# An attention, mixture and MLP kernel on one core: row sums inverted in groups of two head pairs instead of by batch, and two more pairs with split scores

## The chip, the core and the metric

The kernel runs on one core of a Trainium2 chip. Its time is device time in microseconds (us). The core has five engines: TensorE (PE; weight loads are listed apart as PEld), VectorE (DVE), ScalarE (ACT), GpSimd (POOL) and SyncE (SP), which here issues nearly all DMAs. Each engine works through its own instructions in order and waits on semaphores for the others. PE reads from SBUF and writes to PSUM; a DMA moves data between DRAM and SBUF, or inside SBUF.

## What is computed

Three stages follow each other; the output of one is the input of the next.

```python
# 1. attention: q, k, v are [4, 12, 448, 64]
scores = cap * np.tanh(scale * np.matmul(q, k.transpose(0, 1, 3, 2)) / cap)
attn = np.exp(scores - np.max(scores, axis=-1, keepdims=True))
attn = attn / (np.sum(attn, axis=-1, keepdims=True) + 1e-09)
x = np.matmul(attn, v)                    # heads side by side: [4, 448, 768]
# 2. mixture of 4 experts, 2 by token; each is causal attention with 64 columns
a = softmax(where(causal, -1e9, scale * (x @ wq[e]) @ (x @ wk[e]).T))
out += mask[..., None] * w[:, :, kk:kk + 1] * (a @ (x @ wv[e]) @ wo[e])
# 3. gated MLP on out
h = gelu(out @ w_in); u, v = halves(h); v_n = layernorm(v) * g_ln
y = out + (u * (einsum('ts,bsd->btd', w_sg, v_n) + b_sg[None, :, None])) @ w_out
```

The work around the change is the division in the third line of stage 1 and the matrix product of stage 1's first line.

## The kernel before

**Tiling.** There are four batches of 448 tokens (`B`, `S`). Stage 1 goes by pairs of heads: six pairs a batch (`HP`), 24 in all. `slot(i, side)` does pair `i`'s scores beside pair `i-1`'s values. Scores of 128 keys by 448 queries come in blocks; `p` is tanh of a block and then exp, both on ACT. `pb` adds up the blocks of `p` of a pair (DVE, on POOL for some of the later pairs). `values` multiplies `p` by v into `po`, and ACT copies that to `os`, one tile for each group of two pairs.

**The division.** `sums(b, i)` adds up `pb` over its partitions with a matmul by a matrix of ones, for group `i` (0, 1, 2) of batch `b`. With `onehot` it puts the sums of group `i` into row `i` of four blocks of 32 rows, and collects the three groups of a batch in one tile `rs`: ACT copies the first, DVE adds the others. When the batch is complete, `invert` writes `rs` to DRAM (`rd`), `spread` reads it back with four DMAs so that it lies across all partitions (`ri`, 128x42), `inverted` takes the reciprocal on DVE and writes it to DRAM with four DMAs, and `load_rb` reads it twice for each group, repeated over 64 partitions each time (`rb`). `over_sums` multiplies `os` by `rb` on DVE. `in_parts` then makes `xh` (rounded to F32R) and `xl` (what is left), from which stage 2's matmuls `qk` and `v` read. `normed(n, place)` says at which place of which slot each of these steps is recorded.

**Split scores.** From pair `PARTED` on, q and k are first split into a rounded half and a rest (`qh`, `ql`, `kh`, `kl`, in `part`), and a block of scores is three F32R products instead of one in F32 (`block`). The last 64 keys (`tails`) stay in F32 for all pairs.

**What sets the order.** The program is recorded in three parts and each is ordered by a planner in the kernel (`Agenda`): it gives each instruction a duration, lets it start when its inputs, its engine and its buffers are there, and writes every engine's instructions in the order that comes out. Part 1 is slots 0 to 9 with the preparation of `w_in` beside them (`wi` tiles on DVE and ACT, `w2ps` matmuls on PE); part 2 is slots 10 to 24, with stage 2 of the earlier batches beside them (`PLAN`); part 3 is the rest of stage 2 and stage 3. `Agenda.SLACK` is added to each DMA's landing in the first two parts, and `Agenda.MARGIN` (one number for them, one for the third) to what PE waits for from elsewhere. SP's DMAs go by the same plan, so a DMA that waits for a semaphore holds those behind it.

**Other names.** `W_OUT` says at which slots the five first units of `w_out` are prepared, and in which buffers. `experts_end` records the end of stage 2, with the division of the last batch among it. In the rows every operation has line 448, the helper that records them all; the tile names tell them apart.

Of the kernel before, what the change touches and what calls it, by code (L numbers as in the profile page):

```python
# [76 lines left out]
class Agenda:  # L77


    LATENCY = {"pe": 230.0, "act": 60.0, "dve": 60.0, "pool": 100.0, "sp": 60.0}  # L80
    SLACK, MARGIN = 0.0, (0.0, 100.0)
    STATE = ("slots", "queue", "where", "left", "free", "grid", "fresh", "cfg", "bank", "lock", "pipe", "kept")
    RULES = ((100.0, 0.0, 100.0), (100.0, 0.0, None), (100.0, 20.0, 100.0), (60.0, 0.0, 100.0))
    OVERLAP = {"act": 100.0, "dve": 80.0, "pool": 27.0, "sp": 0.0}
# [334 lines left out]
def build(ctx: ExitStack, tc: tile.TileContext, a: dict):  # L419
# [40 lines left out]
    def dma(*args, **kw):  # L460
        return sp.dma_start(*args, **kw) if agenda.on else nc.sync.dma_start(*args, **kw)
# [6 lines left out]

    capt = const.tile([128, 1], F32, name="capt")
    tsc = const.tile([128, 1], F32, name="tsc")  # L470
    onehot = const.tile([128, 3, 32], F32, name="onehot")
    tri = const.tile([128, E, E], F32, name="tri")
    ident = const.tile([128, 128], F32, name="ident")
    mhalf = const.tile([128, 1], F32, name="mhalf")
# [1 line left out]

    def constants(pool):
        negf = pool.tile([128, 128 + KT], F32, name="negf", bufs=1)
        dma(onehot, a["c_onehot"])
        dma(ident, a["c_ident"])  # L480
        dma(negf, a["c_neg"])
        dma(tri, a["c_tri"])
        pool_e.memset(neg, 0.0)
        return negf
# [63 lines left out]
            dma(qp, a["qT"][b, :, hp, :])  # L548
        return qp, kp, load_v(b, hp)

    PARTED = 14

    parts = {}

# [94 lines left out]
    def sums(b, i):  # L649
        g = ps_g.tile([128, 512], F32, tag="g", name=f"sum{b}_{i}")  # L650
        for j in range(4):
            mm(g[32 * j:32 * j + 32, :S], onehot[:, i, :], pend[b, 2 * i + j // 2][2][:, j % 2, :],
                             start=True, stop=True)
        if i == 0:
            sums_t[b] = ao.tile([128, S], F32, name=f"rs{b}", tag="rs", bufs=1)
            act.activation(sums_t[b], g[:, :S], AF.Copy)
        else:
            dve.tensor_tensor(sums_t[b], sums_t[b], g[:, :S], op=ALU.add)
        yield 870.0

    def invert(b):
        d, n = dr.tile([4, 32, S], F32, tag="rd", name=f"rd{b}"), 3 * S // 32
        dma(d.rearrange("j r s -> (j r) s"), sums_t[b])
        rows = d[:, :3, :].rearrange("j r s -> j (r s)").rearrange("j (p c) -> j p c", c=n)
        r = ao.tile([128, n], F32, name=f"ri{b}", tag="ri", bufs=1)
        inv[b] = (r, rows)
        rb_d[b] = d

    def spread(b):
        r, rows = inv[b]  # L670
        for j in range(4):
            dma(r[32 * j:32 * j + 32], rows[j])

    def inverted(b):
        r, rows = inv.pop(b)
        dve.reciprocal(r, r)
        for j in range(4):
            dma(rows[j], r[32 * j:32 * j + 32])

    pairs = [(b, hp) for b in range(B) for hp in range(HP)]  # L680
    ld = {}
# [1 line left out]
    def slot(i, side):  # L683

        if i == 0:
            ld[0] = load_pair(*pairs[0])
            ld[1] = load_pair(*pairs[1])
        if i + 2 < len(pairs):  # L690
            qk = [at.tile([128, n], F32, tag=t, name=f"{t}{i + 2}", bufs=3) for t, n in (("qp", S), ("kp", S + 1))]
            b, hp = pairs[i + 2]
            dma(qk[1][:, :S], a["kT"][b, :, hp, :])
            dma(qk[0], a["qT"][b, :, hp, :])
            ld[i + 2] = qk
        part(i + 1)
        if i < len(pairs):
            first = scores(*pairs[i], 0, *ld[i][:2])
            drain(islice(first, 2))
            side("a")  # L700
            drain(first)
        else:
            side("a")
        side("w")
        if i:
            b, hp = pairs[i - 1]
            drain(values(b, hp, ld.pop(i - 1)[2]))
        if 0 < i < len(pairs) - 1:
            b, hp = pairs[i + 1]
            ld[i + 1] = (*ld[i + 1], load_v(b, hp))  # L710
        side("a")
        if i < len(pairs):
            drain(scores(*pairs[i], 1, *ld[i][:2], None if i % 2 else ld[i + 1][:2]))
        if i == len(pairs):
            drain(sums(B - 1, HP // 2 - 1))
            invert(B - 1)
        side("p")
        if 0 < i < len(pairs):
            b, hp = pairs[i - 1]
            if hp % 2 == 1:  # L720
                drain(sums(b, hp // 2))
        if i < len(pairs):
            add_up(*pairs[i])
        side("n")
# [6 lines left out]
    def load_rb(b, h2, pool=xp, tag=None):  # L731
        rb = rbs[b, h2] = pool.tile([128, 2, S], F32, tag=tag or f"rb{h2 % 2}", name=f"rb{b}_{h2}")
        for r in range(2):
            dma(rb[64 * r:64 * r + 64],
                              rb_d[b][r::2, h2:h2 + 1, :].rearrange("r o s -> o r s").to_broadcast([64, 2, S]))

    def over_sums(b, h2):
        x = os_t[b, h2]
        dve.tensor_mul(x, x, rbs.pop((b, h2)))

    def in_parts(b, h2):
# [8 lines left out]
        if h2 == HP // 2 - 1:  # L750
            for t, y in enumerate((xh, xl)):
                rnd('pv'[t], xr[:, :, t, :], y[:, :, KB * 128:])

    def normed(n, place):

        b = (n - 1) // HP - 1
        step = (n % HP, place)
        if n >= B * HP or b < 0:
            return
        if step == (1, "a0"):  # L760
            invert(b)
        elif step == (1, "w"):
            spread(b)
        elif step == (1, "a1"):
            inverted(b)
        elif step == (2, "w"):
            load_rb(b, 0)
            load_rb(b, 1)
        elif step == (3, "w"):
            over_sums(b, 0)  # L770
            over_sums(b, 1)
            load_rb(b, 2)
        elif b == 0 and step == (3, "a1"):
            in_parts(b, 0)
            in_parts(b, 1)
        elif b == 0 and step == (3, "p"):
            over_sums(b, 2)
            in_parts(b, 2)
        elif b and step == (4, "w"):
            in_parts(b, 0)  # L780
            over_sums(b, 2)
        elif b and step == (4, "a1"):
            in_parts(b, 1)
            in_parts(b, 2)

    projected = []

# [215 lines left out]
    def experts_weights(n, place):  # L1003
# [13 lines left out]
        if place == "w" and n in parts:  # L1017
# [1 line left out]
            rest("v", lo[:, k0:k1, c0:c1], w_raw.pop(n), hi[:, k0:k1, c0:c1])  # L1019


    W_OUT = {11: ("w", xp, "rb0", "rb1"), 14: ("n", at, "ws", "ws"), 17: ("w", at, "ws", "ws"),
             20: ("n", at, "ws", "ws"), 23: ("w", at, "ws", "ws")}
    ws = {n: w_out(*divmod(u, 2), 2, *scratch(*W_OUT[n][1:])) for u, n in enumerate(W_OUT)}

    def beside(n):
# [25 lines left out]
    def experts_end():  # L1052
# [3 lines left out]
        def steps():  # L1056
# [8 lines left out]
            yield from attend(b - 1, 1)  # L1065
            yield from queries_keys(b, 1, 1)
            yield from turn(b, 0, 0)
            over_sums(l, 0)
            over_sums(l, 1)
            yield from weigh(b, 1, 0, 1)  # L1070
            yield from turn(b, 0, 1)
# [333 lines left out]
    v_places = [(ml, "vh", "vl"), (xp, "xh", "xl")] * 2  # L1405
    g_places = [(mg, "gh", "gl"), (mo, "pe2", "pe3"), (mo, "pt"), (mg, "gh", "gl")]
    MLP = 8 * 1278.0 + 8 * 1120.0 + 4 * 1120.0 + 36 * 560.0 + 17.0
    spread(B - 1)
    inverted(B - 1)
    load_rb(B - 1, 0)  # L1410
    load_rb(B - 1, 1)
    load_rb(B - 1, 2, ypool, "y")
    drain(mlp_weights(0))
    C = 36 * 560.0
    drain(experts_end())
# [12 lines left out]
def _layout(x):  # L1428
    q, k, v = x["q"], x["k"], x["v"]
    wide = lambda w: w.transpose(1, 0, 2).reshape(DM, E * HD)  # L1430
    wo = x["moe_wo"].reshape(E * HD, DM)
    out = {
        "qT": q.reshape(B, HP, 2, S, D).transpose(0, 2, 4, 1, 3).reshape(B, 2 * D, HP, S),
        "kT": k.reshape(B, HP, 2, S, D).transpose(0, 2, 4, 1, 3).reshape(B, 2 * D, HP, S),
        "v": v[:, :, :KB * 128].reshape(B, H, KB, 128, D).transpose(0, 3, 1, 2, 4),
        "vt": v[:, :, KB * 128:].reshape(B, HP // 2, 2, 2, KT, D).transpose(0, 1, 2, 4, 3, 5).reshape(B, HP // 2, 2 * KT, 2, D),
        "wqk": _rows(np.concatenate([wide(x["moe_wq"]), wide(x["moe_wk"])], 1)),
        "wvg": _rows(np.concatenate([wide(x["moe_wv"]), x["moe_w_gate"]], 1)),
        "wo": _rows(wo),
        "woT": _rows(wo.T),  # L1440
        "w_in": _rows(x["moe2_w_in"]).view(np.int64),
        "w_out": _rows(x["moe2_w_out"]).view(np.int64),
        "w_sgT": np.concatenate([x["moe2_w_sg"].T, x["moe2_w_sg"].T[KB * 128:]]).reshape(KB + 1, 128, S).transpose(1, 0, 2),
        "g_ln": x["moe2_g_ln"].reshape(4, 128).T,
        "b_sg": x["moe2_b_sg"].reshape(1, S),
    }
    out["k_cap"] = np.concatenate([out["kT"][0, :, 0, :], np.full((2 * D, 1), x["cap"], np.float32)], 1)
    hot = np.zeros((128, 3, 32), np.float32)
    for i in range(3):
        hot[:, i, i] = 1.0  # L1450
    hot[:, 0, 3:] = 1.0
    e, r = np.arange(E), np.arange(128)
    above = lambda n: np.where(np.arange(n)[None, :] > (r % n)[:, None], -1e9, 0.0)
    out["c_ident"] = np.eye(128, dtype=np.float32)
    out["c_onehot"] = hot
    out["c_tri"] = np.broadcast_to((e[None, :] < e[:, None]).astype(np.float32), (128, E, E))
    out["c_neg"] = np.concatenate([above(128), above(KT)], 1).astype(np.float32)
    return {n: np.ascontiguousarray(w) for n, w in out.items()}
# [17 lines left out]
```

## Time and profile before

| | |
|---|---|
| time, median of 3 runs | 499.27 us (495.3 to 501.08) |
| the profiled execution | 497.36 us, span 495.6 us |
| PE busy | 484.4 us, 98% of the span |
| DVE busy | 354.0 us, 71% |
| ACT busy | 325.7 us, 66% |
| POOL busy | 98.7 us, 20% |
| granted TensorE clock | 0.998 of full speed |

The span is the time from the first to the last instruction. A matmul's records overlap the next one's, so what a group of matmuls costs is read from its start to the start of the next group. "Idle before" is how long an engine stood before an instruction, with what ended the idleness behind the arrow. For a DMA the row on SP is its issue; it lands later.

### The profile page before, as it was taken

The numbers are of one execution on the slowest core, as the hardware profiler recorded it, in microseconds if no ns is written. First come the engines' busy times: TensorE is split into PE (matmuls) and PEld (weight loads), VectorE is DVE, ScalarE is ACT, GpSimd is POOL, SyncE is SP. The second block draws the span as 40 slices with busy tenths as digits, with TensorE's granted clock in tenths as the row PEclk, the third lists the DMA queues.
The fourth block names the chain that finished last, engine by engine and source line by source line (L and its number), as shares of the span: only waits on it lengthen the run. The fifth ranks groups of instructions, "written<-read, shape, count | busy, mean of one in ns | idle before, by whom it ended". The sixth has DMA issues, their size and how long they took to land.

```text
span 495.6 us, 7599 instructions
## 1 busy us (share of the span) xinstructions
PE 484.4 (98%) x2711; PEld 330.8 (67%) x2711; DVE 354.0 (71%) x736; ACT 325.7 (66%) x553; POOL 98.7 (20%) x106
## 2 busy tenths in 40 slices
PE   8999999899999999999999999999999999999996
PEld 3333333354756556656558897687898998999996
DVE  4999975599878798778863999835987949806000
ACT  6999978879779878688836776747554635513211
POOL 0000000054162444264261302033010100100000
PEclk9999999999999999999999999999999999999999
DMA  8984535855255304142045621152001110110112
GB/s 296 361 288 140 182 101 163 202 156 154 90 143 148 112 22 158 43 139 89 2 136 176 176 60 54 55 202 86 1 1 37 38 38 1 56 57 19 57 74 74
DMA packets 35525, 54.34 MB, mean 110 GB/s; under 512 B 5408, under 2 KB 30496, under 8 KB 35488
## 3 DMA queue, kind: packets, MB, share of 16 engines
q1 hardware_dynamic: 35056, 53.52, 34.4%
q8 instruction: 21, 0.34, 0.3%
q10 hardware_dynamic: 432, 0.34, 0.2%
q14 instruction: 16, 0.13, 0.1%
HBM read 42.10 MB, written 11.75 MB: 109 GB/s over the span
## 4 chain that ended last, share of the span: by engine, by line
PE 87%; ACT 4%; DMA 3%; DVE 2%; issue 1%; SPq 1%; ACTq 0%; DVEq 0%
PE o L448 18%; PE po L448 12%; PE qk L448 11%; PE s L448 10%; PE sp L448 7%; PE v L448 7%; PE a L448 4%; PE hu L448 4%; PE hv L448 4%; PE w2ps L448 4%; DMA rb<-rd 3%; PE tr L448 3%; PE av L448 2%; ACT p L448 2%; PE sum L448 2%
## 5 line engine op out<-in xcount | busy, mean ns | idle before, releaser
L448 ACT ACTIVATE p<-s,tsc 128x896 f32<-128x896 f32 (+1 forms) x85 | 82.0, 999 | 15.6 <-PE s L448 15.4
L448 ACT ACTIVATE p<-p,capt 128x1792 f32<-128x1792 f32 (+1 forms) x48 | 77.3, 1610 | 0.6
L448 DVE TENSOR_TENSOR pb<-pb,p 128x896 f32<-128x896 f32 (+1 forms) x48 | 57.7, 1203 | 8.2 <-ACT p L448 5.6
L448 PE MATMUL po<-p,vv 128*64 128x448 f32 x288 | 59.9, 548 | 0.5 <-ACT p L448 0.5
L448 PE MATMUL s<-qp,kp 64*128 64x448 f32 (+2 forms) x268 | 50.5, 561 | 0.7 <-ACT p L448 0.7
L448 DVE CUSTOM_DVE_ANT_0 a<-a,neg 128x128 f32<-128x128 f32 (+3 forms) x56 | 24.9, 467 | 25.6 <-PE a L448 23.7
L448 POOL TENSOR_TENSOR pb<-p 128x896 f32<-128x896 f32 x14 | 33.7, 2413 | 47.0 <-ACT p L448 36.7
L448 PEld LDWEIGHTS po<-p,vv 128*64 128x64 f32 x288 | 18.3, 136 | 36.7 <-issue 30.8
L448 PE MATMUL qk<-xh,wqk_h 128*128 128x448 f32 x96 | 36.8, 383 | 3.6 <-DVE xh L448 3.5
L448 ACT ACTIVATE ob<-o 128x448 f32<-128x448 f32 (+1 forms) x24 | 12.6, 532 | 38.9 <-PE o L448 35.4
L448 PEld LDWEIGHTS s<-qp,kp 64*128 64x128 f32 (+1 forms) x268 | 18.7, 172 | 28.4 <-issue 17.8
L448 PE MATMUL qk<-xh,wqk_l 128*128 128x448 f32 x96 | 34.9, 364 | 0.0
L448 ACT ACTIVATE pe<-a,m 128x128 f32<-128x128 f32 (+3 forms) x56 | 27.4, 496 | 11.4 <-DVE m L448 8.8
L448 DVE SCALAR_TENSOR_TENSOR vs<-sp,gln,bsg 128x448 f32<-128x448 f32 x16 | 10.6, 680 | 30.2 <-PE sp L448 30.0
L448 POOL TENSOR_TENSOR rstd<-rstd,mhalf 128x1 f32<-128x1 f32 (+1 forms) x16 | 10.9, 683 | 98.3 <-DVE rstd L448 98.3
L448 POOL TENSOR_SCALAR pe<-pe,cs 128x128 f32<-128x128 f32 (+4 forms) x40 | 23.1, 590 | 23.4 <-DVE cs L448 22.7
L448 PEld LDWEIGHTS qk<-xh,wqk_h 128*128 128x128 f32 x96 | 18.0, 187 | 13.3 <-DVE xh L448 5.6
L448 POOL TENSOR_SCALAR xr<-xh 128x384 fp32r<-128x384 f32 x4 | 3.7, 927 | 113.3 <-DVE xh L448 107.4
L448 PE MATMUL a<-qk 64*128 64x128 f32 (+3 forms) x128 | 24.0, 449 | 0.7 <-ACT qk L448 0.6
L448 ACT ACTIVATE gsu<-gsu 128x448 f32<-128x448 f32 x16 | 9.3, 579 | 23.2 <-DVE gsu L448 22.9
L448 PE MATMUL sp<-sg_h,vh 128*128 128x448 f32 x64 | 23.7, 370 | 0.0
L448 PE MATMUL sp<-sg_l,vh 128*128 128x448 f32 x64 | 23.4, 366 | 0.0
(272 smaller groups left out, 1234.0 us busy)
## 6 DMA issues: line engine op xcount, KB each, us to landing
rb<-rd SPq DMA_DIRECT2D x24, 224.0 KB, 6.4
kp<-in_kT_dram SPq DMA_DIRECT2D x23, 224.0 KB, 4.2
qp<-in_qT_dram SPq DMA_DIRECT2D x23, 224.0 KB, 4.4
out_dram<-ob SPq DMA_DIRECT2D x23, 224.0 KB, 1.9
vv<-in_v_dram SPq DMA_DIRECT2D x24, 192.0 KB, 3.3
wuw<-in_w_out_dram SPq DMA_DIRECT2D x5, 384.0 KB, 3.8
wud<-wuw SPq DMA_DIRECT2D x10, 192.0 KB, 2.6
ws<-in_wqk_dram SPq DMA_DIRECT2D x4, 384.0 KB, 5.2
```

The lines of the kernel that those rows point to most:

```text
L448: return tc.keep_in_program_order(f(*args, **kw))
```

## The change

The sums of a group no longer wait for the batch. `sums` uses a plain matrix of ones, and each group has an `rs` of its own (ACT copies group 0, DVE groups 1 and 2). `spread` takes one row of each block of 32 and spreads it over 32 partitions with a DMA from SBUF to SBUF, so the first trip through DRAM is gone. `inverted` takes the reciprocal of 128x14 and writes it to DRAM with one DMA, and `load_rb` and `over_sums` follow for that group. `NORM` records the steps at fixed distances behind the group's last pair: spread and reciprocal one slot behind the slot of its sums, `rb` one further, the multiplication one further. For the last batch only the last group is left for the end. `PARTED` goes from 14 to 12, so pairs 12 and 13 have split scores as well. `SLACK` goes from 0 to 1000 ns, and the third part's `MARGIN` from 100 to 200 ns. The units of `w_out` move from slots 11, 14, 17, 20, 23 to 14, 16, 18, 20, 23, with other buffers for one of them.

```diff
-    SLACK, MARGIN = 0.0, (0.0, 100.0)
+    SLACK, MARGIN = 1000.0, (0.0, 200.0)
...
-        dma(onehot, a["c_onehot"])
+        pool_e.memset(ones, 1.0)
...
-    PARTED = 14
+    PARTED = 12
...
-            mm(g[32 * j:32 * j + 32, :S], onehot[:, i, :], pend[b, 2 * i + j // 2][2][:, j % 2, :],
-                             start=True, stop=True)
-        if i == 0:
-            sums_t[b] = ao.tile([128, S], F32, name=f"rs{b}", tag="rs", bufs=1)
-            act.activation(sums_t[b], g[:, :S], AF.Copy)
-        else:
-            dve.tensor_tensor(sums_t[b], sums_t[b], g[:, :S], op=ALU.add)
+            mm(g[32 * j:32 * j + 32, :S], ones, pend[b, 2 * i + j // 2][2][:, j % 2, :], start=True, stop=True)
+        rs = sums_t[b, i] = ao.tile([128, S], F32, name=f"rs{b}_{i}", tag="rs", bufs=1)
+        rnd("avv"[i], rs, g[:, :S])
         yield 870.0
 
-    def invert(b):
-        d, n = dr.tile([4, 32, S], F32, tag="rd", name=f"rd{b}"), 3 * S // 32
-        dma(d.rearrange("j r s -> (j r) s"), sums_t[b])
...
-    def spread(b):
-        r, rows = inv[b]
+    def spread(b, i):
+        rs = sums_t.pop((b, i))
+        r = inv[b, i] = ao.tile([128, S // 32], F32, name=f"ri{b}_{i}", tag="ri", bufs=2)
         for j in range(4):
-            dma(r[32 * j:32 * j + 32], rows[j])
-
-    def inverted(b):
-        r, rows = inv.pop(b)
+            dma(r[32 * j:32 * j + 32], rs[32 * j:32 * j + 1].rearrange("o (q c) -> o q c", q=32))
+
+    def inverted(b, i):
+        r = inv.pop((b, i))
         dve.reciprocal(r, r)
-        for j in range(4):
-            dma(rows[j], r[32 * j:32 * j + 32])
+        d = rb_d[b, i] = dr.tile([4, S], F32, tag="rd", name=f"rd{b}_{i}", bufs=4)
+        dma(d.rearrange("j (q c) -> (j q) c", q=32), r)
...
+    NORM = {(1, "w"): spread, (1, "a1"): inverted, (2, "w"): load_rb, (3, "w"): over_sums}
+    PARTS = {(9, 'w'): 0, (9, 'a1'): 1, (9, 'p'): 2}
...
+        for b in range(B):
+            for i in range(HP // 2):
+                f = NORM.get((n - b * HP - 2 * i - 2, place))
+                if f:
+                    f(b, i)
...
-    W_OUT = {11: ("w", xp, "rb0", "rb1"), 14: ("n", at, "ws", "ws"), 17: ("w", at, "ws", "ws"),
-             20: ("n", at, "ws", "ws"), 23: ("w", at, "ws", "ws")}
+    W_OUT = {14: ('n', at, 'ws', 'ws'), 16: ('n', at, 'ws', 'ws'), 18: ('n', at, 'ws', 'ws'), 20: ('n', at, 'ws', 'ws'), 23: ('w', at, 'ws', 'ws')}
...
-    spread(B - 1)
-    inverted(B - 1)
-    load_rb(B - 1, 0)
-    load_rb(B - 1, 1)
-    load_rb(B - 1, 2, ypool, "y")
+    inverted(B - 1, HP // 2 - 1)
+    load_rb(B - 1, HP // 2 - 1)
```

What the planner makes of it shows at three places. In the names the numbers behind a tile are batch, pair or group, and a running number. The first place is PE at the first use of batch 0's normed output, before: after a block of scores of batch 1's pair 4 come four matmuls `qk` of batch 0, then the tails of the scores and the next pair's first block, and then further `qk`.

```order
L448 MATMUL s1_4_2_809<-qp10_256,kp10_257 128x448 x2
L448 MATMUL qk0_0_0_812<-xh0_286,wqk_h_76 128x448
L448 MATMUL qk0_0_0_812<-xh0_286,wqk_l_77 128x448
L448 MATMUL qk0_0_0_812<-xh0_286,wqk_h_76 128x448
L448 MATMUL qk0_0_0_812<-xh0_286,wqk_l_77 128x448
L448 MATMUL s1_4_3_810<-qp10_256,kp10_257 64x448 x2
L448 MATMUL s1_4_3_810<-qp11_275,kp11_276 64x448 x2
L448 MATMUL s1_5_0_819<-qp11_275,kp11_276 128x448 x2
L448 MATMUL qk0_0_0_812<-xh0_286,wqk_h_76 128x448
```

Now twelve `qk` with `xh` follow the same block of scores without a break; their last row, and what comes behind, is this.

```order
L448 MATMUL qk0_0_0_835<-xh0_290,wqk_l_77 128x448
L448 MATMUL qk0_0_0_835<-xl0_291,wqk_h_76 128x448 x6
L448 MATMUL s1_4_3_833<-qp10_264,kp10_265 64x448 x2
L448 MATMUL s1_4_3_833<-qp11_282,kp11_283 64x448 x2
L448 MATMUL sum1_1_836<-pb1_2_271,ones_71 32x448 x2
L448 MATMUL sum1_1_836<-pb1_3_287,ones_71 32x448 x2
L448 MATMUL s1_5_0_845<-qp11_282,kp11_283 128x448 x2
```

The 18 `qk` stand in one run, ahead of the tails that stood among them. The second place is DVE at batch 0's division, before: the reciprocal of the whole batch, sums of `p` for batch 1, and then, interleaved with the rest of these, the three multiplications `os0` and the splits `xh` and `xl`.

```order
L448 RECIPROCAL ri0_246<-ri0_246 128x42
L448 TENSOR_TENSOR pb1_2_263<-p1_2_0_258 128x896
L448 TENSOR_TENSOR pb1_2_263<-pb1_2_263,p1_2_1_270 128x896
L448 TENSOR_TENSOR pb1_2_263<-pb1_2_263,p1_2_1_270 64x896
L448 TENSOR_TENSOR pb1_3_280<-p1_3_0_277 128x896
L448 TENSOR_TENSOR os0_1_157<-os0_1_157,rb0_0_265 128x896
L448 TENSOR_TENSOR pb1_3_280<-pb1_3_280,p1_3_1_289 128x896
L448 CAST xh0_286<-os0_1_157 128x896
L448 TENSOR_TENSOR os0_3_193<-os0_3_193,rb0_1_266 128x896
L448 TENSOR_TENSOR xl0_287<-os0_1_157,xh0_286 128x896
```

Now `os0_1` and `os0_3` are multiplied earlier (beside `wi8m` and `wi10m`), and the splits of these two stand ahead of the sums for pair 2 of batch 1, the last group's multiplication among them.

```order
L448 CAST xh0_290<-os0_3_196 128x896
L448 TENSOR_TENSOR w2l1_1_302<-w2ps1_1_243,w2h1_1_301 128x512
L448 TENSOR_TENSOR xl0_291<-os0_3_196,xh0_290 128x896
L448 TENSOR_TENSOR pb1_2_271<-p1_2_0_266 128x896
L448 TENSOR_TENSOR pb1_2_271<-pb1_2_271,p1_2_1_277 128x896
L448 TENSOR_TENSOR os0_5_237<-os0_5_237,rb0_2_273 128x896
L448 TENSOR_TENSOR pb1_2_271<-pb1_2_271,p1_2_1_277 64x896
L448 CAST xh0_290<-os0_5_237 128x896
L448 TENSOR_TENSOR xl0_291<-os0_5_237,xh0_290 128x896
L448 TENSOR_TENSOR pb1_3_287<-p1_3_0_284 128x896
```

The last group's multiplication has moved ahead of pair 3's first sum; before, it was the last of the three and stood behind all of pair 3's. The third place is SP's queue of DMAs there, before: the batch's trip back from DRAM, loads and stores, the reciprocals to DRAM, and `rb` of two groups behind six other DMAs.

```order
L448 DMA ri0_246<-rd0_245 32x42 x4
L448 DMA qp10_256<-in_qT_dram 128x448
L448 DMA w2d0_82<-w2h1_0_291 128x512
L448 DMA w2d1_83<-w2l1_0_292 128x512
L448 DMA rd0_245<-ri0_246 32x42 x4
L448 DMA kp11_276<-in_kT_dram 128x448
L448 DMA qp11_275<-in_qT_dram 128x448
L448 DMA vt1_4_285<-in_vt_dram 128x128
L448 DMA w2d0_82<-w2h1_1_293 128x512
L448 DMA vv1_4_284<-in_v_dram 128x384
L448 DMA w2d1_83<-w2l1_1_294 128x512
L448 DMA rb0_0_265<-rd0_245 64x2x448 x2
```

Now, for group 2 of the same batch:

```order
L448 DMA ri0_2_255<-rs0_2_245 32x1x14 x4
L448 DMA vv1_3_276<-in_v_dram 128x384
L448 DMA ws9_288<-in_wvg_dram 128x780
L448 DMA kp10_265<-in_kT_dram 128x448
L448 DMA qp10_264<-in_qT_dram 128x448
L448 DMA rd0_2_261<-ri0_2_255 128x14
L448 DMA w2d0_82<-w2h1_0_299 128x512
L448 DMA rb0_2_273<-rd0_2_261 64x2x448 x2
L448 DMA kp11_283<-in_kT_dram 128x448
```

The last group's `rb` now goes ahead of `kp11` and the four loads and stores that stood before it.

## Rows read from the trace of the kernel before

**Rows 1.** The page: busy us (share of span), then DVE's busy tenths in 40 slices.
```profile
PE 484.4 (98%) x2711; PEld 330.8 (67%) x2711; DVE 354.0 (71%) x736; ACT 325.7 (66%) x553; POOL 98.7 (20%) x106
DVE  4999975599878798778863999835987949806000
```
**Rows 2.** PE's waits: who waited <- for whom: us in total, times, longest.
```profile
PE qk L448 <- DVE xh L448: 3.5, 2, 2.3
...
PE s L448 <- ACT p L448: 0.7, 2, 0.5
PE a L448 <- ACT qk L448: 0.6, 1, 0.6
...
PE tr L448 <- DVE vp L448: 0.3, 1, 0.3
PE v L448 <- ACT pe L448: 0.2, 1, 0.2
```
**Rows 3.** Timeline of PE, 60 to 130 us: start us, us, operation, [idle before <- what ended it].
```profile
61.25 1.02 PE L448 MATMUL w2ps<-wi9m,wt 128*128 128x512 f32 x2
62.11 1.02 PE L448 MATMUL w2ps<-wi6m,wt 128*128 128x512 f32 x2
...
65.64 0.96 PE L448 MATMUL sum<-pb,onehot 128*32 128x448 f32 x8
...
91.86 1.77 PE L448 MATMUL s<-qp,kp 64*128 64x448 f32 x8
95.97 0.47 PE L448 MATMUL qk<-xh,wqk_h 128*128 128x448 f32 x1 [2.33 <-DVE xh L448]
...
103.68 0.47 PE L448 MATMUL qk<-xh,wqk_h 128*128 128x448 f32 x1 [1.16 <-DVE xh L448]
```
**Rows 4.** Timeline of all engines, 68 to 112 us, the same columns.
```profile
73.93 0.42 SPq L448 DMA_DIRECT2D qp<-in_qT_dram  x1
...
84.06 2.61 SPq L448 DMA_DIRECT2D rb<-rd  x4
...
86.74 1.77 PE L448 MATMUL s<-qp,kp 64*128 64x448 f32 x8
...
93.28 1.09 DVE L448 TENSOR_TENSOR os<-os,rb 128x896 f32<-128x896 f32 x1 [3.22 <-DMA rb<-rd]
...
95.29 0.62 DVE L448 CAST xh<-os 128x896 fp32r<-128x896 f32 x1
...
98.06 1.92 ACT L448 ACTIVATE p<-s,tsc 128x896 f32<-128x896 f32 x2 [1.55 <-PE s L448]
...
101.87 1.09 DVE L448 TENSOR_TENSOR os<-os,rb 128x896 f32<-128x896 f32 x1 [1.10 <-DMA rb<-rd]
```
**Rows 5.** The page: the chain that ended last, share of the span by line.
```profile
PE o L448 18%; PE po L448 12%; PE qk L448 11%; PE s L448 10%; PE sp L448 7%; PE v L448 7%; PE a L448 4%; PE hu L448 4%; PE hv L448 4%; PE w2ps L448 4%; DMA rb<-rd 3%; PE tr L448 3%; PE av L448 2%; ACT p L448 2%; PE sum L448 2%
```
**Rows 6.** The tile `rb`: from issue to landing of its DMAs.
```profile
DMA to landing us min/median/max: 4.1/6.4/9.7
```
**Rows 7.** The tile `ri`: from issue to landing of its small DMAs.
```profile
DMA to landing us min/median/max: 1.3/1.9/3.4
```
**Rows 8.** The page: DMAs by line, count, KB each, median us to landing.
```profile
qp<-in_qT_dram SPq DMA_DIRECT2D x23, 224.0 KB, 4.4
```
**Rows 9.** The chain in order of time: start us, us, piece (scores, F32, then halves).
```profile
50.00 1.70 PE s L448 x8
...
147.27 1.41 PE s L448 x12
```
**Rows 10.** Groups of DVE by shape: count | busy us, mean ns | idle before.
```profile
L448 DVE TENSOR_TENSOR kl<-kp,kh 128x448 fp32r<-128x448 f32 x10 | 9.1, 911 | 1.3 <-ACT kh L448 1.3
...
L448 DVE TENSOR_TENSOR rs<-rs,sum 128x448 f32<-128x448 f32 x8 | 4.9, 617 | 2.4 <-PE sum L448 2.2
...
L448 DVE RECIPROCAL ri<-ri 128x42 f32<-128x42 f32 x4 | 1.6, 406 | 0.0
```
**Rows 11.** Timeline of DVE, 24 to 70 us.
```profile
60.07 0.69 DVE L448 TENSOR_TENSOR wi9m<-wi9m,wi9e 128x512 f32<-128x512 f32 x1
```

## What was predicted before the run

> **What bounds the kernel now.** I read the page's busy shares first, then the PE's list of waits, then the timeline at the place where that list puts most of its time, and last the chain. The PE is busy for 484.4 of 495.6 us [rows 1], so the time is the PE's own work, and only what the PE waits for can be given back. Its list is short: 3.5 us for `xh`, then 0.7, 0.6, 0.3 and 0.2 [rows 2]; two entries from the start of the program are left out. The 3.5 us lie at one place, the first use of batch 0's normed output. The PE ends the scores that it began at 91.86, 1.77 us long, stands 2.33 us until 95.97, and later 1.16 us until 103.68 [rows 3]. What is late there is `xh`, the cast of the attention output after its division by the row sums. DVE begins the first multiplication by `rb` at 93.28, after 3.22 us of idleness that a DMA `rb<-rd` ended, casts at 95.29, and begins the last multiplication at 101.87, released by that DMA again [rows 4]. The page's chain gives these DMAs 3% of the span [rows 5], some 15 us, and a reader could take that for the prize. It is not: while they ran, the PE mostly had other work, and it stood for 3.49 us.
>
> **The change, part by part.**
>
> *Sums by groups.* Before, all six pairs of a batch were summed before anything was inverted: one DMA to DRAM, four back, a reciprocal, four to DRAM, then `rb` for the groups. Now each group of two pairs goes its own way: four DMAs from SBUF to SBUF, a reciprocal of 14 columns instead of 42, one DMA to DRAM and two `rb` DMAs. For batch 0 the question is when group 2, the last, is ready. Its sum matmuls keep their place in the PE's order and end at 65.64 + 0.96 = 66.6 [rows 3]. Ahead of their copy DVE has two multiplications more (1.09 us each, the row at 93.28) and two reciprocals (under 0.41 each [rows 10]); with the copy itself (0.62, the row of the addition that it replaces [rows 10]) it is there by 66.6 + 2.2 + 0.8 + 0.6 = 70.2. Four spreads are issued in at most 2.6 us, as four `rb` DMAs are at 84.06 [rows 4], and land 1.3 to 3.4 us later [rows 7]: at most 76.2. The reciprocal takes it to 76.6. The DMA of its result stands in SP's queue behind `qp`, which went out at 73.93 [rows 4], and lands by 80; `rb` leaves by 81 and lands 4.1 to 9.7 us later [rows 6]: 85 to 91. Multiplication and cast (1.09 and 0.62) make `xh` 87 to 92.5. The PE wants it at 91.86 + 1.77 = 93.6, and groups 0 and 1 stand ahead of group 2 in DVE's order. So both waits go: **-3.49 us**, bounds 0 (`rb` is late after all) and -3.49.
>
> *Sums elsewhere.* `ones` for `onehot` leaves the matmuls as many and as wide. A batch keeps three passes over 448 columns on ACT and DVE, now copies instead of additions, and has three reciprocals for one. It has 21 DMAs instead of 15, 24 more in all; at up to 0.65 us each (2.61 for four at 84.06) these are 16 us of SP, spread over some 200 us, and hidden as long as SP's queue runs ahead. The cover: `qp` went out at 73.93, takes a median of 4.4 us to land [rows 8] and is first read in the scores that begin at 86.74 [rows 4], so some 8 us may be lost before the PE sees it. Cost 0; without that cover, whatever a group holds SP beyond 8 us.
>
> *Two more pairs with split scores.* Pairs 12 and 13 form scores from halves in F32R. Two blocks of F32, eight matmul instructions, take 1.70 us; two blocks from halves, twelve, take 1.41 [rows 9]. With three blocks for each of two pairs that is 3 x 0.29 = **-0.87 us** on the PE, bounds 0 and -0.87. Making the halves costs DVE a cast and two subtractions for each pair, under 0.91 us each by the row of `kl` [rows 10], and ACT a cast. They lie between 95 and 135 us, where DVE has lost three multiplications, casts and subtractions (3 x (1.09 + 0.62 + 1.09) = 8.4 us) to the stretch before. Hidden; with the cover gone, at most 6 x 0.91 = 5.5 us of DVE.
>
> *The stretch in which DVE is full.* Up to 62 us DVE stands at nine tenths or more [rows 1]. One multiplication, two reciprocals and a pass of `pb` (1.09) come ahead of the last step of `wi9m` there, 3.0 us. Before, that step ends at 60.07 + 0.69 [rows 11] and the PE reads it at 61.25 [rows 3], half a microsecond later. The new order puts that product three places of 0.86 us later on the PE (61.25 to 62.11), which nearly pays. I take **+0.2**, bounds 0 and 3.0 - 0.5 = +2.5.
>
> *Planner's numbers.* The first two plans now take every landing as 1 us later, and the last takes what comes from another engine as 0.1 us later for the PE. In the last part the PE waits 0.6 + 0.3 + 0.2 = 1.1 us in all [rows 2], and its order is unchanged from the middle of the MLP on. I take **-0.3**, bounds -1.1 (all of it) and +1.1 (as much again). The units of `w_out` at other slots move POOL and DVE work, with POOL busy for 20% [rows 1]: 0; cover gone, a unit's few us, once.
>
> *What is late next.* When the PE no longer stands 3.5 us for `xh`, ACT and DVE lose 3.5 us in which they caught up. ACT itself stood 1.55 us for scores just then (98.06 [rows 4]), so it was not behind, but the sum leaves something for it: **+0.5**, bounds 0 and +2.5.
>
> Sum: -3.49 - 0.87 + 0.2 - 0.3 + 0.5 = **-4.0 us**. The profiled execution took 497.36 us (the span and 1.8 around it), so 493.4; the median of the three runs is 499.27, so 495.3. With three runs to one the base is 498.8, and the forecast **494.8 us**.
>
> **The rivals.**
>
> *The idle time comes back as another wait.* What follows 103 us was ordered by a plan; with 3.5 us less of slack, ACT's `exp` may be what ends last before the scores and the values. For it: 0.7 us of waiting for ACT's `p` is there already [rows 2]. Against it: ACT waited for the PE at 98.06. Then the scores' 0.87 and some 0.6 of the waits remain, -1.5: 497.3 us.
>
> *All waits go.* The longer reserves take all 1.1 us at the end as well: -3.49 - 0.87 - 1.1 = -5.5: 493.3 us. For it: a reserve is made for such short waits. Against it: the longest of them, for `qk` from ACT, stands in rows that the PE's order keeps.
>
> *SP's queue becomes the bound.* Each group adds points at which SP stands still, for the copy, the reciprocal and the landing of `rd`, with the loads of q, k and v queued behind. If a group holds SP longer than the 8 us of room, the PE waits for a load. At 0.8 us in each of 11 groups that is +8.8 - 4.0 = +4.8: 503.6 us; it makes the kernel slower from 0.36 us a group on. Against it: the small DMAs land in at most 3.4 us [rows 7], and before had such points too, once a batch. The Trainium skill, DMA: Bandwidth & Descriptors (Rules for kernel authors), speaks for it: many small transfers should be made one, because under 64 KB one pays mostly overhead. By that rule at its strictest, with all 24 of them on the path at 0.65 us, the sum would be +11.6 instead of -4.0 us. That a small one is mostly overhead, the 1.3 to 3.4 us of before agree with; that the PE would see it, no row shows.
>
> **How the numbers follow.** A measurement of this kernel can tell about 1%, 5 us, from no change. Forecast 0.55, the wait that comes back 0.22, all waits gone 0.16, SP's queue 0.07. The forecast lies close to the line at 1% (499.27 less 5.0 is 494.3) and single runs spread by some 3 us: 0.42 of the forecast falls below the line, nearly all of "all waits go" and little of the rest, 0.23 + 0.15 + 0.02 = 0.40 faster. Slower by over 1% is most of SP's case, 0.05, and the other 0.55 lies within 1%. The range runs from 493.3 less 2.8 of spread, 490.5, to 497.3 and 1.7, 499.0.
>
> **What would show it.** Right: no wait of `qk` for `xh` above 0.3 us, and the first `qk` of batch 0 as one run of 18 matmuls; no wait of `os` for `rb` above 1 us; scores from halves in pairs 12 and 13 at 0.71 us a block; the PE's list of waits shorter by its 3.5 us. Wrong: a new entry of over 1 us in that list (for `p`, `pb`, a `wi` or a load), or SP standing for `ri` so long that q and k land just before they are read.

## The result and the profile after

The changed kernel takes **493.62 us** (median of 10 runs, 493.34 to 494.44), the kernel before 498.61 (10 runs, 495.3 to 501.08): a ratio of 0.991, 95% interval 0.9886 to 0.9934. That is 5.0 us faster, where 4.0 were forecast. The two profiled executions differ by less: 497.36 us before, 494.44 after, 2.9 us. The kernel before was profiled in one of its shorter executions, the changed one in its longest.

The page of after has for [rows 1]:

```profile
PE 483.9 (98%) x2723; PEld 332.1 (67%) x2723; DVE 351.9 (71%) x750; ACT 324.6 (66%) x555; POOL 98.7 (20%) x107
```

PE's list of waits, for [rows 2] (who waited, for whom, us in total, times, longest):

```profile
PE warm L448 <- DVE tsc L448: 1.0, 1, 1.0
PE s L448 <- ACT p L448: 0.9, 2, 0.5
PE s L448 <- DMA qp<-in_qT_dram: 0.7, 1, 0.7
PE a L448 <- ACT qk L448: 0.6, 1, 0.6
PE a L448 <- ACT pt L448: 0.6, 1, 0.6
PE tr L448 <- DVE vp L448: 0.3, 1, 0.3
PE po L448 <- ACT p L448: 0.2, 1, 0.2
PE v L448 <- ACT pe L448: 0.2, 1, 0.2
```

The 3.5 us for `xh` are gone. PE's timeline at the same place, for [rows 3] (start us, us, operation): `qk` follows the scores without a pause, and all 18 of its matmuls stand together, up to 99.43.

```profile
93.88 1.77 PE L448 MATMUL s<-qp,kp 64*128 64x448 f32 x8
95.59 0.47 PE L448 MATMUL qk<-xh,wqk_h 128*128 128x448 f32 x1
95.90 0.37 PE L448 MATMUL qk<-xh,wqk_l 128*128 128x448 f32 x1
...
98.12 1.37 PE L448 MATMUL qk<-xl,wqk_h 128*128 128x448 f32 x6
99.43 0.98 PE L448 MATMUL s<-qp,kp 64*64 64x448 f32 x8
```

The tile `rb` in the trace of after, for [rows 6]:

```profile
L448 DVE TENSOR_TENSOR os<-os,rb x12: 1076/1084/1109, 50.9 to 273.1; 128x896 f32<-128x896 f32 x12
...
  DMA rb<-rd: 1.9, 1
...
DMA to landing us min/median/max: 3.5/4.1/6.0
```

DVE still waited for `rb` once, 1.9 us before the multiplication at 257.8 us, but the first multiplication starts at 50.9 us instead of 93.3, and PE saw nothing of that wait.

To compare kernels I use two quantities of PE, whose sum is nearly the whole span. Its **idle** time is the sum of the pauses between the end of one matmul and the start of the next. **Busy** is the page's figure: what the list of matmuls takes in the order in which it stands. Before had 6.3 us idle and 484.4 busy, after 4.0 and 483.9. Of the 3.5 us of waiting that went, 1.2 came back in small pieces, the longest of them 0.7 for `qp` at 9.4 us and 0.6 for `pt` at 296.

### The profile page after: what moved, and what is told of

Same layout as the page of the kernel before. It is cut to its first block, busy times and chain, and to the rows that moved or that the text cites. A ratio compares the mean times of both kernels' runs of the same rounds, so it can differ in the third digit from the quotient of the medians.

```text
span 492.7 us, 7686 instructions
## 1 busy us (share of the span) xinstructions
PE 483.9 (98%) x2723; PEld 332.1 (67%) x2723; DVE 351.9 (71%) x750; ACT 324.6 (66%) x555; POOL 98.7 (20%) x107
## 4 chain that ended last, share of the span: by engine, by line
PE 85%; DMA 4%; DVE 4%; ACT 4%; issue 1%; SPq 0%; ACTq 0%; DVEq 0%
PE o L448 18%; PE qk L448 12%; PE po L448 10%; PE s L448 9%; PE sp L448 7%; PE v L448 7%; PE a L448 4%; PE hv L448 4%; PE hu L448 4%; PE av L448 3%; PE tr L448 3%; ACT p L448 3%; PE w2ps L448 2%; DVE pb L448 2%; PE sum L448 2%; DMA wi_5w<-in_w_in_dram 1%
## 5 line engine op out<-in xcount | busy, mean ns | idle before, releaser
L448 DVE TENSOR_TENSOR pb<-pb,p 128x896 f32<-128x896 f32 (+1 forms) x48 | 52.8, 1099 | 9.0 <-ACT p L448 8.3
L448 PE MATMUL s<-qp,kp 64*128 64x448 f32 (+2 forms) x244 | 45.7, 560 | 1.5 <-ACT p L448 0.9
L448 POOL TENSOR_TENSOR pb<-p 128x896 f32<-128x896 f32 x14 | 31.6, 2260 | 58.1 <-ACT p L448 37.2
L448 PEld LDWEIGHTS s<-qp,kp 64*128 64x128 f32 (+1 forms) x244 | 16.0, 168 | 28.7 <-issue 12.6
L448 POOL TENSOR_SCALAR pe<-pe,cs 128x128 f32<-128x128 f32 (+4 forms) x40 | 24.4, 622 | 42.1 <-DVE cs L448 41.2
L448 PE MATMUL qk<-xl,wqk_h 128*128 128x448 f32 x96 | 22.0, 364 | 0.0
```

The lines of the kernel that those rows point to most:

```text
L448: return tc.keep_in_program_order(f(*args, **kw))
```

## The experiments

All runs together; "shapes" is how often the list of matmuls changes from one tile shape to another, idle and busy are those of the profiled execution, and the ratio is against runs of the kernel before on the same chip in the same session (497.8, 497.4 and 497.9 us in the three sessions). Where kernels of different sessions are set side by side below, their ratios are the safer measure. The reserves are the planner's `SLACK` and the third part's `MARGIN`; "reserve 300" is a `SLACK` of 300 ns.

| kernel | shapes | idle | busy | median us | ratio, 95% interval |
|---|---|---|---|---|---|
| before | 152 | 6.3 | 484.4 | 498.6 | 1 |
| changed | 151 | 4.0 | 483.9 | 493.6 | 0.991 (0.9886 to 0.9934) |
| groups alone | 154 | 5.9 | 485.6 | 498.0 | 1.0004 (0.9984 to 1.0023) |
| split alone | 168 | 7.5 | 487.1 | 501.9 | 1.0079 (1.0049 to 1.0110) |
| reserves alone | 167 | 5.0 | 487.6 | 498.6 | 0.9999 (0.9978 to 1.0019) |
| groups and reserves, split as before | 156 | 3.1 | 485.0 | 495.2 | 0.9947 (0.9918 to 0.9977) |
| changed, reserve 0 | 154 | 8.8 | 485.1 | 499.5 | 1.0042 (1.0022 to 1.0062) |
| changed, reserve 100 | 154 | 5.3 | 483.5 | 494.0 | 0.9923 (0.9890 to 0.9956) |
| changed, reserve 300 | 152 | 2.5 | 483.0 | 492.4 | 0.9876 (0.9829 to 0.9924) |
| before, reserve 300 | 158 | 5.7 | 486.6 | 500.4 | 1.0053 (1.0018 to 1.0087) |
| reserves alone, dearer shape | 152 | 15.2 | 493.1 | 512.7 | 1.0318 (1.0282 to 1.0354) |
| changed, dearer shape | 146 | 10.6 | 487.5 | 504.7 | 1.0152 (1.0122 to 1.0183) |
| groups alone, dearer shape | 145 | 13.1 | 489.7 | 506.1 | 1.0163 (1.0125 to 1.0201) |

**The parts, one by one.** My theory was that the groups remove the wait and bring 3.5 us by themselves, the split 0.9, the reserves little. The rival was that the idle time comes back elsewhere.

Groups alone (the changed kernel with the planner's numbers and the pair of the split as before):

```diff
-    SLACK, MARGIN = 1000.0, (0.0, 200.0)
+    SLACK, MARGIN = 0.0, (0.0, 100.0)
-    PARTED = 12
+    PARTED = 14
```

> The changed kernel with the split scores back at pair 14 and the planner's reserves back at 0 and 100 ns: only the sums by groups (and the slots of w_out that go with them) are new. If the groups carry the gain by taking the 3.5 us wait for xh away: 494 to 495 us, no wait of qk for xh above 0.3 us. If the reserves carry it: 497.5 to 499 us. If the long DMA rb<-rd is also what spreads the times of the kernel before (495.3 to 501.1), the spread of this one falls below 1 us.

Measured: 497.99 us, nothing gained, and its runs still scatter by 2.0 us. The wait for `xh` is indeed gone. PE's waits in this run begin with two others in its place:

```profile
PE po L448 <- ACT p L448: 2.0, 4, 0.9
PE s L448 <- ACT p L448: 1.2, 3, 0.5
```

Together 3.2 us for ACT's `p`, where before and the changed kernel have 1.1 each. These are seven short waits, all before 97 us; busy time is 1.2 us more. So the rival of the wait that comes back holds for this part taken alone.

Split alone (before with `PARTED` 12):

```diff
-    PARTED = 14
+    PARTED = 12
```

> The kernel before with split scores from pair 12 and nothing else. By six blocks at 0.29 us for two: 0.87 us less than before, 497.7 us. By the rival that blocks of these pairs stand singly between other matmuls, so that each pays for its own start: no gain, 498.6 us. The wait of qk for xh stays, and with it the spread of several us, if that wait is what spreads.

Measured: 501.87, 4.1 us slower than before, where neither theory had a loss. Idle is 1.2 us more and busy 2.7, with 168 changes of shape for 152.

Reserves alone (before with the new planner's numbers):

```diff
-    SLACK, MARGIN = 0.0, (0.0, 100.0)
+    SLACK, MARGIN = 1000.0, (0.0, 200.0)
```

> The kernel before with the planner's SLACK at 1000 and the last MARGIN at 200 ns, the division by batch. If the plan only has to know of late landings, it puts other work in front of the first qk: the wait for xh falls from 3.5 to about 1 us and the time to 495.5 us. If the division by batch is late whatever the order is: 498 to 499 us and xh still waited for by 2 us or more.

Measured: 498.58, no change. The wait for `xh` goes here too, although the chain through DRAM is the old one. The timeline of PE in this run shows how it was bought off:

```profile
97.62 0.47 PE L448 MATMUL qk<-xh,wqk_h 128*128 128x448 f32 x1
97.93 0.36 PE L448 MATMUL qk<-xh,wqk_l 128*128 128x448 f32 x1
98.13 0.36 PE L448 MATMUL qk<-xh,wqk_h 128*128 128x448 f32 x1
...
98.62 0.96 PE L448 MATMUL sum<-pb,onehot 128*32 128x448 f32 x8
99.51 1.02 PE L448 MATMUL s<-qp,kp 64*128 64x448 f32 x4
100.47 0.47 PE L448 MATMUL qk<-xh,wqk_h 128*128 128x448 f32 x1
...
101.47 2.48 PE L448 MATMUL po<-p,vv 128*64 128x448 f32 x12
103.88 1.02 PE L448 MATMUL s<-qp,kp 64*128 64x448 f32 x4
104.83 0.47 PE L448 MATMUL qk<-xh,wqk_h 128*128 128x448 f32 x1
```

`qk` is cut into runs of four with other work between them, and the scores into single blocks. Each piece pays for its start. Read from start to next start, two blocks of scores together take 1.71 us (93.88 to 95.59 in the changed kernel above), two single ones 0.96 and 0.95, and the first `qk` of a run takes 0.31 us where the next takes 0.20. Over the whole program that is 15 more changes of shape and 3.2 us more of busy time, at a granted clock of 1.00 for as long as PE works, which eats the 1.3 us of idle time saved and more. The split alone pays alike: 16 changes, 2.7 us. From these two a change of shape costs some 0.2 us, but the count is a rough guide only: kernels with 151 to 154 changes lie between 483.0 and 485.6, and one with 152, below, at 493.1 with a part of it at a slower clock.

Groups and reserves, with the split from pair 14 as before (an edit of the changed kernel):

```diff
-    PARTED = 12
+    PARTED = 14
```

> The changed kernel with the split scores back at pair 14. If the two further pairs give 0.87 us: 494.5 us against 493.6. If they give nothing, as the lone blocks suggest: 493.4 to 493.8 us.

Measured: 495.16, above both theories, whose 493.6 comes from another session. Against the reserves alone (498.58, same chip and session) the groups are worth 3.4 us. That is the price that the prediction gave them, but not for its reason: neither of these two kernels waits for `xh`, and between their profiled executions 2.6 us are busy time and 1.9 idle. Of this, 0.9 us lies in the last part (from the first `v` behind the last sums PE takes 234.3 us with the reserves alone, 233.4 here), which the prediction's price left out. Without the reserves the same groups are worth nothing. "The groups" always includes the new slots of `w_out`, which were never tried apart.

**Does the reserve do it?** The changed kernel with `SLACK` 0:

```diff
-    SLACK, MARGIN = 1000.0, (0.0, 200.0)
+    SLACK, MARGIN = 0.0, (0.0, 200.0)
```

> The changed kernel with the reserve for transfers taken back alone: SLACK 0 in place of 1000, groups of two pairs and split scores from pair 12 stay. Its list of matmuls changes tile shape 154 times (151 with the reserve). Theory of the order (PE's time is its idle time plus what the order costs it, about 0.19 us for each change of tile shape, the slope between the kernels so far): the wait for xh stays away, since the groups alone already removed it, but waits of up to 1 us for ACT p come back as in the run with the groups alone; idle 5 to 6 us instead of 3.9, busy time +0.6: 495.5 to 497. Rival, the groups are what removed the wait and the reserve does nothing of its own: 493.6 as the changed kernel.

Measured: 499.47, worse than both theories said. Idle is 8.8 us, 3.7 of them for ACT's `p` before 97 us, then 0.9 for POOL at 149 and 1.0 for DVE's `ql` at 176. Either transfers need the reserve, or a reserve of 0 merely tips the planner into a bad list. Two sizes between help to tell these apart, 100 and 300 in place of the 1000:

```diff
-    SLACK, MARGIN = 1000.0, (0.0, 200.0)
+    SLACK, MARGIN = 100.0, (0.0, 200.0)
```

> The changed kernel with a reserve of 100 ns in place of 1000 (SLACK). With none at all the run gave 499.5 and seven waits of PE for ACT p in the first 97 us, 3.5 us together. Theory of the accident: a reserve of 0 merely tipped the greedy planner into a worse list for the first 97 us; with 100 the list there begins like that of the changed kernel, so these waits go, PE's idle time is 4 to 5 us and the time 493 to 495. Rival, the reserve itself is needed: 100 ns is a tenth of it, the waits for ACT p, ql and pe (2 us at 149 and 176 us in the run with none) stay: 497 to 499.5.

> The changed kernel with a reserve of 300 ns in place of 1000; its list of matmuls differs from that of the changed kernel in few places (152 changes of tile shape against 151). Theory of the accident: as the changed kernel or half a microsecond less, 493.0 to 493.8, as nothing in the changed kernel's trace uses the full 1000. Rival, transfers land later than planned and the full reserve is needed: waits for DMA or for what hangs on one (xh, os) of over 0.5 us, 495 or more.

Measured: 494.01 and **492.36** (492.05 to 492.82). A tenth of the reserve gives 5.5 of the 5.9 us back (between sessions), and three tenths give more than all of it. That speaks for the list: transfers that need 1000 ns would not do with 100. With 100 the seven waits for ACT's `p` are down to two of 2.1 us, 1.6 of them at 27.9 us. With 300 the list of PE's waits is the shortest of all:

```profile
PE warm L448 <- DVE tsc L448: 1.0, 1, 1.0
PE a L448 <- ACT qk L448: 0.6, 1, 0.6
PE a L448 <- ACT pt L448: 0.6, 1, 0.6
PE s L448 <- ACT p L448: 0.4, 1, 0.4
PE tr L448 <- DVE vp L448: 0.3, 1, 0.3
PE v L448 <- ACT pe L448: 0.2, 1, 0.2
```

This version is faster than the kernel before, and its slowest run is 0.5 us below the fastest of the changed kernel. That last margin is between two sessions, and the intervals of the two ratios overlap, so it is not shown that 300 is better than 1000.

Is the gain of the groups an accident of lists as well? The old chain with a reserve of 300:

```diff
-    SLACK, MARGIN = 0.0, (0.0, 100.0)
+    SLACK, MARGIN = 300.0, (0.0, 200.0)
```

> The kernel before (sums of all six pairs through DRAM, split from pair 14) with a reserve of 300 ns and the margin of 200. The reserve of 1000 gave 498.6, without the wait for xh but with 15 more changes of tile shape and 3.1 us more of PE's busy time. This list has 158 changes, 6 more than before. Theory that the late chain costs about 3 us whichever way it is paid (as a wait for xh, or as work put in front of it in a worse order): wait for xh 1 to 3 us, busy 484.4 + 6 x 0.19 = 485.5, time 497 to 498.5. Rival, the loss of the reserves alone was an accident of one list: wait for xh under 1 us and busy under 485, 494 to 495.5.

Measured: 500.43 (498.92 to 505.6), above both. PE waits 1.1 us for `xh`, and busy is 2.2 us more than before. But 1.8 us of its time stand in the last part (235.3 us against 233.5 before), where batch 0's chain plays no role, so the run does not price that chain alone. The old chain gave 497.8, 500.4 and 498.6 with reserves of 0, 300 and 1000. The groups gave 499.5, 494.0, 492.4 and 493.6 with 0, 100, 300 and 1000 and the earlier split, 498.0 with 0 and 495.2 with 1000 without it. With the planner's rules as they are, no list tried with the old chain has a median below 497, and of the groups' lists with any reserve none is above 495.2. With equal settings the groups bring nothing at a reserve of 0 and the old split (498.0 against 497.8), 2.4 us at 0 and the earlier split (499.5 against 501.9, between sessions), and 3.4 at 1000 and the old split. So the gain over the kernel before belongs to the groups and a reserve together, and neither alone brings any. Both of the groups' lists with 0 have the same seven waits for `p` before 97 us; why the planner makes them so is not shown.

**Fewer changes of shape.** If pieces cost, a planner that avoids them should gain. `RULES` holds the charge for a matmul of another shape when the next one is chosen; the planner makes a list by each entry and keeps the one that it takes to be shortest. I raised the charge to 300 ns and left out the entry that charges nothing.

```diff
-    RULES = ((100.0, 0.0, 100.0), (100.0, 0.0, None), (100.0, 20.0, 100.0), (60.0, 0.0, 100.0))
+    RULES = ((100.0, 0.0, 300.0), (100.0, 20.0, 300.0), (60.0, 0.0, 300.0))
```

> The kernel before with the reserves, as in the run with the reserves alone (498.6), and one more thing: the planner charges 300 ns instead of 100 for a matmul of another tile shape when it chooses the next one (RULES, without its second entry, which charges nothing). The list of matmuls then changes shape 152 times instead of 167. Theory of the order: PE's busy time falls by 15 x 0.19 = 2.9 us from 487.55 to about 484.7, idle stays near 5 us: 495.7. Rival, the shape changes are not what costs and the busy time of the run with the reserves has another cause: busy stays at 487.5 and the time at 498.6.

> The changed kernel with the same dearer charge for another tile shape: 146 changes of shape instead of 151. Theory of the order: busy -5 x 0.19 = -0.95 us, 492.7, if no wait over 0.5 us comes in for it. Rival, the planner gives up readiness for fewer changes: PE's idle time rises by as much or more, 493.6 to 495.

> The groups alone (kernel before with the sums inverted in groups of two pairs, reserves and pair of the split as before; 498.0) with the same dearer charge: 145 changes of shape instead of 154. Theory of the order: busy -9 x 0.19 = -1.7 us, 496.3. Rival, as in the run of the groups alone the loss sits in waits for ACT p: 498.0 or more.

All three are slower than the kernels that they started from, by 8 to 14 us: 512.73, 504.74 and 506.07. No theory had named losses of that size. The shapes did become fewer, but PE's idle time rose by 6.7 to 10.2 us and its busy time too. In the second run PE ends 241.0 us after the first `v` behind the last sums (the start of the last part), against 233.4 in the changed kernel. The edit did two things at once, a dearer charge and one entry less, so it doesn't tell which of them spoilt that stretch, and the price of a change of shape was not measured by it. It showed another price: the windows of the second run around its longest pause, 1.90 us up to 336.06 (stretch us, its length, PE busy us (matmuls), granted clock, DMA share, GB/s):

```profile
332.00:334.00 2.00, 2.00 (x16) 1.00 0.00 0
334.00:336.00 2.00, 0.16 (x2) 1.00 0.00 0
336.00:338.00 2.00, 1.94 (x11) 0.98 0.01 4
338.00:340.00 2.00, 1.86 (x6) 0.50 0.00 0
340.00:342.00 2.00, 2.00 (x16) 0.67 0.00 0
342.00:344.00 2.00, 2.00 (x10) 1.00 0.00 0
```

Behind the pause the granted clock goes to 0.50, the 1.2 GHz level. The three stretches of 2 us from 336 to 342 us lack the shares 0.02, 0.50 and 0.33 of the full clock, together 1.7 us of it, which is 3.4 us at half of it. A long wait can be paid twice.

**The scatter of the kernel before.** The same kernel, profiled once more, since its runs lie 5.8 us apart:

> The kernel before once more, for a second profile, since its runs lie 5.8 us apart (495.3 to 501.1) and those of the changed kernel 1.1. Theory that the scatter is the chain through DRAM: where the time is longer than the 497.4 of the first profile, the difference stands in the waits for xh and os. Rival, it stands elsewhere, in the granted clock or in the waits for qp and p in the first 30 us.

Measured: 499.56 us, 2.2 more than the first profile. Matmul by matmul PE is 2.1 us later than in the first profile from 35 us on: a wait for the DMA of `qp` at 9.8 us and longer waits for `p` at 27 and 32. Then comes the wait for `xh`, 2.10 us, shorter than in the first profile, and behind it the clock. PE's windows in this profile:

```profile
96.00:98.00 2.00, 0.15 (x1) 1.00 0.96 301
98.00:100.00 2.00, 2.00 (x12) 0.79 0.68 186
100.00:102.00 2.00, 2.00 (x8) 0.50 0.91 228
102.00:104.00 2.00, 2.00 (x14) 0.86 0.57 199
104.00:106.00 2.00, 2.00 (x13) 1.00 0.59 166
```

and in the first profile, behind a longer pause of 2.33 us [rows 3]:

```profile
94.00:96.00 2.00, 0.04 (x1) 1.00 0.93 283
96.00:98.00 2.00, 2.00 (x14) 1.00 0.85 184
98.00:100.00 2.00, 2.00 (x12) 1.00 1.01 245
```

The slow clock put PE another 1.6 us behind, and the wait of 1.16 us at 103.68 [rows 3] vanished, since `xh` had caught up meanwhile. Behind that place PE is 2.25 us later than in the first profile, and 2.2 at its end. So the theory failed and the rival holds: the two profiles differ by the loads and the waits for `p` of the first 35 us, the waits for `xh` were shorter in the longer execution, and 1.2 of the 1.6 us that the clock took came back in the second wait.

Of 50 further runs of the kernel before, the 14 with a mean granted clock of 0.997 or less took 499.2 us on average, the other 36 took 497.4. These were not profiled, and a mean below 1.00 need not come out of PE's work. The first profile's 0.998 does not; its windows show the slow clock only behind PE's last matmul:

```profile
488.00:492.00 4.00, 3.66 (x19) 1.00 0.25 86
492.00:496.00 4.00, 0.00 (x0) 0.75 0.24 86
```

How often the wait for `xh` costs the clock, and whether that makes runs longer in the end, stays open. So does why the groups with a reserve of 300 or 1000 scatter by only 0.7 to 1.1 us (4 to 10 runs each), where groups alone and reserves alone scatter by 2.0.

## Why the prediction was right, and where it was not

**The groups' chain.** The chain of times held, nearly every step of it early. For group 2 of batch 0 the sums end at 67.1 us (66.6 forecast), `ri`'s reciprocal starts at 74.6 (76.2), `rb` is issued at 78.6 (81), and `xh` is there at 89.8 (87 to 92.5), against 95.6 when PE wants it. The small DMAs from SBUF land in 1.4 to 4.6 us, median 1.8, much as those through DRAM did [rows 7]. But "so both waits go: -3.49 us" passed from the wait to the time too quickly: the wait also goes with the reserves alone, and the time stays, because the list pays. With the planner's numbers alike for both (reserve 1000, split as before) the groups are worth 3.4 us, by busy and idle time and not by a wait for `xh`. That this is so near to 3.49 is luck.

**The split scores.** This step held in its place and failed in the whole. The -0.87 took a block from F32 at 0.85 us and one from halves at 0.705, from pairs of blocks [rows 9]. By starts of matmuls, less pauses, the six blocks of pairs 12 and 13 take some 5.0 us before and 4.4 after, 0.74 a block. (That is an estimate: where a block from halves follows one in F32 without a change of shape, they are told apart by these two prices.) But all scores together take 70.7 us before and 70.9 after: the blocks from pair 14 on, which the edit doesn't touch, take some 0.7 us more, two of them standing singly at 129.07 and 138.50 us with 0.81 and 0.80, and the tails take 0.4 more. The earlier split still goes with a faster kernel, 493.6 against 495.2, with 5 fewer changes of shape and 1.1 us less of busy time (`qk`, `a` and `po` 1.3 less). But these are two sessions, the intervals of the two ratios overlap, and the two profiled executions differ by 0.2 us, so a gain of the split is not shown. In the old list the same edit cost 4.1 us. What it brings is decided by the list.

**The planner's numbers.** -0.3 with bounds of 1.1 was the step that was most too small. It was sized by the waits of the last part, for which the margin is meant. There nothing moved: from the first `v` behind the last sums PE takes 233.5 us before and 233.4 after, and with the groups alone, whose margin is the old one, 233.4 too. It is the reserve in the first 255 us that counts, 499.5 to 492.4 us between four sizes of it. The largest effect of this change was one that I had treated as a detail, and it is no term of its own: alone the reserves bring nothing.

**DVE's full stretch, what is late next, SP's queue.** 0.2 and 0.5 were forecast; the products of `wi` take 0.5 us more than before, and 1.2 us of waiting came back. Both were too small, and so on the same side as the split's 0.9, of which the scores as a whole show nothing. (DVE's nine tenths hold from 12 us on; its first slice in [rows 1] shows four.) The 24 more DMAs cost PE nothing that its waits show: its one wait for a load, at 9.4 us, comes before the first of them, at 31.4. The Trainium skill, DMA: Bandwidth & Descriptors (Rules for kernel authors), would have them made into larger ones. The trace shows 0.6 us of SP for each, and no wait of PE for one of them.

**The sum against the time.** -3.5 of wait, +1.2 of other waits and -0.5 of busy time make 2.8 of the 2.9 us between the two profiles, where 4.0 were forecast. Busy time fell although the scores and the products of `wi` missed their terms, because `qk`, `a`, `tr` and `av` take 1.3 us less in the new list, which no term had. The other 2.1 us up to the medians are which executions were profiled; the base of 498.8, between the one profile and the three runs, allowed for that, and is why the forecast of 494.8 lay near 493.6. So the wait and the direction were right, and the nearness of the number is in part luck.

**The rivals.** "The idle time comes back" is what the groups alone do (497.3 given, 498.0 measured), not the whole change. "All waits go" gave 493.3, and the time is there, but not by its mechanism: its 1.1 us were to come from the last part. Those 1.1 us of waiting stand in the last part of the changed kernel as before, and with a reserve of 300 too. SP's queue never showed. Of the signs, the vanished wait for `xh` and the one run of 18 `qk` came as said, and no new wait of over 1 us; but PE's waits are 2.3 us shorter instead of 3.5, and `os` did wait for `rb` once, 1.9 us.

## What to carry to other kernels

In a kernel whose order a planner writes, a part of a change must not be priced by the wait that it removes: the edit changes the list, and lists of the same work differed here by some 8 us of PE's busy and idle time (reserves of 0 and 300). Price the wait and the list apart (pauses of the bounding engine, and its busy time with its runs and changes of shape), and try a few sizes of the planner's reserve before giving a part up or taking credit for it. The shortened chain took PE's wait for `xh` away in every list here, and made the kernel faster than before only in lists made with a reserve.

## What the runs showed of the hardware

Behind pauses of PE of 1.90, 1.91, 2.01 and 2.10 us, in four profiles (the three of the dearer shape and the second of the kernel before), the granted clock stood at 0.50, which is 1.2 GHz, for some 3.4 us each, worked out from the windows as above. The program of before did this behind 2.10 us and not behind 2.33, and the groups with the dearer shape not behind 1.87 us at 27 us. In two of the three profiles of the dearer shape a stretch of 6.8 us at 0.50 began in the second of two shorter pauses, of 1.3 and 1.3 to 1.5 us, some 3 us apart; the third, with 1.28 and 1.48 us, stays at 1.00 there. So it is not the length of the pause alone, and single profiles of one kernel can differ by it. It took 1.6 us of PE's time at one place here. The Trainium skill, TensorE: Matmul & The Clock Gate (Part 1: The HAM clock gate), says that an idle array goes to half its rate. The trace agrees in the level, 0.50, and shows that behind a pause of like length it may also stay at 1.00.
